# One TensorE-filled kernel, linear attention and a mixture of experts, with its steps in another listed order

## The chip, the cores and the metric

The program runs on one core of a Trainium2 chip. A core has five instruction streams that matter here: TensorE (PE, matmuls into PSUM), VectorE (DVE), ScalarE (ACT), GpSimd (POOL) and SyncE (SP, which only issues transfers). Each works through its own list in order and waits on semaphores for the others. The metric is the device time of one execution in microseconds (us); the time of the kernel before is the median of three runs.

## The reference

For 8 batches of 8 heads, 576 positions and 64 values a head, a linear attention is computed with an exponential feature map of 128 features and its negative. Its output, as 512 values a position, goes through four attention experts with a causal softmax, of which two are chosen and weighted per position. Cut to what is computed:

```
def phi(x):
    proj = einsum('bhsd,df->bhsf', x, w_phi)
    proj = proj - max(abs(proj), axis=-1)
    return concatenate([exp(proj), exp(-proj)])
q_p, k_p = phi(q), phi(k)
kv, z = einsum('bhsf,bhsd->bhfd', k_p, v), sum(k_p, axis=2)
x = (q_p @ kv) / (q_p @ z + 1e-6)            # to [8, 576, 512]
w = softmax over the 2 largest of x @ w_gate
for e in range(4):
    q, k, v = x @ wq[e], x @ wk[e], x @ wv[e]
    a = softmax(causal(q @ k.T / 8))
    out += (w of e) * (a @ v @ wo[e])
```

## The kernel before

Two heads make a pair; there are 32 pairs, four a batch. Every piece of work is a Python generator that yields a `Step` for each instruction or group of instructions that it wants to issue, with the engine it needs, and where it takes a PSUM bank, the tag of the bank. `Plan.loop` (L214) goes through the string `ORDER`: each character names the generator that issues its next step. Where a step may run on ScalarE or VectorE, the string `SIDES` says on which. So the order on each engine is written out by hand, character by character, and `in_order` (L237) ties every engine to it. There are eight PSUM banks of 512 columns, `PSUM_TILES = (("c", 8, 512),)`, and every step of TensorE takes its output bank from them; the bank is free again when the step that empties it has been issued.

The steps on TensorE and their tile shapes, rows by columns of the array, as the traces name them:

- `keep_warm` (L456, matmuls at L294): 21 small matmuls of the tile `warm`, in seven steps of three, into a bank that nobody reads. Shape 128*128.
- `stream_k` and `stream_tails` (L501): projections of a pair's keys (`k_in`, 16 matmuls into two banks) and of the last 64 keys of two pairs (`kt_in`, four matmuls). `stream_q` (L501): projections of queries (`q_in`, four matmuls of 256 and four of 320 columns into four banks). All 64*128.
- `tail_products` (L607, L615): 64*32. `stream_kv` (L642 with `v_in`, L654): keys times values and key sums, 128*32, then transposes at L665, 128*128.
- `stream_n` (L740 denominators, L751 numerators), `sums` (L1038), `attend` (L1067), `gates` (L961): 128*32.
- `proj_t` (`x` with `qk`), `proj_v` (`x` with `vg`) and `out_unit` (`yh`, `yl` with `wo`), all at L294: 128*128.
- `scores` (L871): 64*128, the last 64 keys in 64*64.

A matmul of two `F32` operands stands in the trace as two, one of `F32R` operands (L294, L871) as one. The banks are emptied by VectorE (maximum L566, subtraction L569, copies L315, products and remainders) and ScalarE (copies L303, exponentials L305). Loads go through SP's queue (L327) in the listed order; the first two pairs' queries go through ScalarE's queue. Single buffers, `v_in` among them, are loaded again when their last reader on TensorE is through.

The planner in the file keeps a model of engine times, and `change_cost` in it adds a cost when the shape on TensorE changes. With the order fixed by `ORDER`, that model decides only which free bank a step gets: the one that has been free longest by its times.

Of the kernel before, what the change touches and what calls it, by code (L numbers as in the profile page):

```python
# [17 lines left out]
DM, E = 512, 4  # L18
# [23 lines left out]
LAST = 7  # L42
# [3 lines left out]
WARM = 0   # L46
# [17 lines left out]
def change_cost(a, b):  # L64
# [12 lines left out]
    r'CG8D?5=B<GH6C4:99B2ECMEBEJA8J9886=GJD?>778CMI<HJKI>I<I@<BG39E9C18IHE<A@=8=?E?9G8857?7?EHAJJF083882HGF8ICDHC8DD'
    r'998:C6:GJHI>?I<:JG<1J:7IGH7J:KJGD:?<<BB:BE>@C>;GIIF>L;8>GJGIIJ;8<:=8:HJGHGGJ:IF::LGGK?I=N8=5:=>@K802GQJMM>F:I<'
    r':<0CEEBK=CFE::CFDCDDCJBICDCJCE=D9;;IJHJ<ICIKFHDF4883DD<8<G<<=BBBEI=CCDCDGEFEHGE8BB8D6A8>:I<C5:@@JJ@JEECIAD6BFI'
    r':JK:9FLH9MCLCIJGDHAF9BFAHD8IHBCIE880DH=28BHCB9;ADA@@CA@C@AEL@HB=ECD9;JJBBJD<BGFC;38772J7GF88GG?K=FD<CF895?==A3'  # L80
    r'=8EB888E67FE18D@KHJ@<0E@BCB28=E9988BBDIJID8DGB8848AF<B6<6EE57:7::G=HICLHE3DJDI:::;<BJGC>HD9GHG>B>GADEAF>EEE=8D'
    r'880@C?=B:98:DAF6DIEH8G8GBD9<:::GHHG7BB?NICL5H7B6N=EE;BGC@FI;G=E9?BDJEEBA:<::MGKKDBCG:GC=CD@BIGLMGKFBJH<G:=1348'
    r'8>?EI8IHCA=B;C<<<B>B28>:8:>>>JD>DL8DCBFKJE8::C=<FKEA5G8@:<=HFJHH9<>99AM=6HD?EK==K3@88028K7CJCLFNMKD>?<F?8G887?'
    r'26I88I<AGCC?KJBG<?G=99?8F>H?>F88883AH?E9=I5=F170GIJ@EIKG<=A<DE=HE<7LDB9=<M808<;;C<C6FDCDA99<GGDJ8G@KK7DL85N2GB'
    r'38JGNMGNMHFE?GAG6F><<7:::48E:FF8F8CDFB=E:E:FIJKJ>8FCCCI89B9JIBHI>8:FDDC@D88A::EA3D7F:LFHK8:<II7PHFG?A?@KL@H=5B'
    r'KNN8:6::MPOAMAOGE;E:80:F28E241AKLIJIIFAEEB08=B>ECE8EF:;;89GHH8@@>?5HE6?HI?IHCFBE?B<<<<<GE6BDB>AC?E=CBCB?>:9;@9'
# [179 lines left out]
def tile_linear_attn_moe(ctx, tc, qt, kt, v, wts, out):  # L266
# [925 lines left out]
```

## Time and profile before

| | us |
|---|---|
| median of three runs | 585.22 |
| lowest and highest of them | 584.14, 585.57 |
| profiled execution: span from its first to its last instruction | 582.0 |
| TensorE busy | 568.9 |
| VectorE busy | 533.0 |
| ScalarE busy | 454.3 |
| GpSimd busy | 290.3 |

The profile shows one execution. Its span is what the page counts from the first to the last instruction; the run's time holds some more on both sides, 3.2 us if this execution took what the median did. Busy time is the union of an engine's instructions. In the timeline a piece is a series of like instructions; its start is measured, while the end of a matmul is modelled and contains the drain, so the time that a piece takes from the stream is read from its start to the start of the next piece.

### The profile page before, as it was taken

The page shows a single profiled execution, that of the slowest core. Times are in us where ns is not written, and L with a number is a line of the kernel's source. Part 1 is how long each engine was busy: PE and PEld are TensorE (multiplying, and loading weights), DVE is VectorE, ACT ScalarE, POOL GpSimd, SP SyncE. Part 2 cuts the span into 40 slices and gives each one's busy share as a digit, 9 for nine tenths or more (in the row PEclk, how much of TensorE's full clock was granted, in tenths as well). Part 3 has the DMA queues.
Part 4 walks back from the last instruction along what each step waited for, and adds up shares of the span by engine and source line. Part 5 has one row for each costly group of instructions (what it writes and reads, how often), then busy time and mean ns, then how long its engine had stood idle before and what let it go on. Part 6 is the DMA issues. An engine that isn't in the chain of part 4 may idle for free.

```text
span 582.0 us, 19187 instructions
## 1 busy us (share of the span) xinstructions
PE 568.9 (98%) x7655; PEld 439.9 (76%) x7655; DVE 533.0 (92%) x1150; ACT 454.3 (78%) x1109; POOL 290.3 (50%) x223
## 2 busy tenths in 40 slices
PE   7998999999999999999999999999999999999997
PEld 5664797678785779667876878867888677878886
DVE  7999899999999998999898989989999998898894
ACT  4999888878897969868878877979778678677562
POOL 3737472666336474465554466446635367331430
PEclk9999999999999999999999999999999999999999
DMA  6579656653445753593664663565646432311012
GB/s 164 151 180 212 119 119 141 148 116 95 95 122 136 180 121 55 139 229 76 153 139 102 156 133 107 100 156 134 131 125 148 116 87 46 89 57 43 1 56 110
DMA packets 55049, 69.74 MB, mean 120 GB/s; under 512 B 29232, under 2 KB 32688, under 8 KB 54960
## 3 DMA queue, kind: packets, MB, share of 16 engines
q1 hardware_dynamic: 48368, 49.58, 29.3%
q0 software_dynamic: 6272, 18.35, 19.9%
q8 instruction: 60, 0.98, 0.7%
q10 hardware_dynamic: 320, 0.59, 0.4%
q14 instruction: 29, 0.24, 0.1%
HBM read 35.59 MB, written 14.55 MB: 86 GB/s over the span
## 4 chain that ended last, share of the span: by engine, by line
PE 86%; DVE 6%; DMA 4%; ACT 2%; issue 1%; SPq 0%; ACTq 0%; DVEq 0%
PE ps_c L294 31%; PE ps_c L501 10%; PE ps_c L751 10%; PE ps_c L642 10%; PE ps_c L1067 7%; PE ps_c L871 7%; PE ps_c L740 5%; DMA v_in<-in_v_dram 2%; PE ps_c L654 2%; PE ps_c L607 2%; DVE s L1000 1%; DMA q_in<-in_qt_dram 1%; PE ps_c L1038 1%; DVE u L715 1%; DVE max L1012 1%
## 5 line engine op out<-in xcount | busy, mean ns | idle before, releaser
L713 POOL PARTITION_ALL_REDUCE mx<-u x64 | 145.1, 2289 | 68.2 <-DVE s L1000 17.5
L294 PE MATMUL ps_c<-x,qk 128*128 128x256 f32 (+1 forms) x768 | 108.0, 298 | 0.6 <-DVE yl L298 0.6
L294 PEld LDWEIGHTS ps_c<-x,qk 128*128 128x128 f32 x768 | 102.7, 189 | 4.4 <-issue 0.9
L996 POOL PARTITION_ALL_REDUCE max<-top x16 | 57.7, 3605 | 39.3 <-DVE top L992 18.1
L979 POOL TENSOR_SCALAR_AFFINE_SELECT s<-s 128x256 f32<-128x256 f32 (+1 forms) x80 | 46.4, 626 | 57.3 <-ACT s L303 45.3
L305 ACT ACTIVATE ek<-ek 128x1024 f32<-128x1024 f32 x64 | 67.9, 1061 | 8.0 <-DVE ek L569 7.3
L303 ACT COPY s<-ps_c 64x64 f32<-64x64 f32 (+4 forms) x141 | 52.9, 434 | 17.7 <-PE ps_c L871 17.4
L1000 DVE TENSOR_TENSOR s<-s,max 128x1152 f32<-128x1152 f32 (+4 forms) x80 | 65.5, 853 | 0.6 <-POOL max L996 0.6
L642 PE MATMUL ps_c<-ek,v_in 128*32 128x256 f32 x1024 | 61.7, 381 | 2.2 <-DMA v_in<-in_v_dram 2.2
L305 ACT ACTIVATE s<-s 128x384 f32<-128x384 f32 (+4 forms) x80 | 57.7, 742 | 7.4 <-DVE s L1000 7.1
L294 PE MATMUL ps_c<-yh,wo 128*128 128x256 f32 (+1 forms) x256 | 52.9, 300 | 0.0
L331 POOL DMA_DIRECT2D zs<-ekt x28 | 23.7, 845 | 58.3 <-DVE zs L582 22.4
L642 PEld LDWEIGHTS ps_c<-ek,v_in 128*32 128x32 f32 x1024 | 31.5, 110 | 25.4 <-DMA v_in<-in_v_dram 2.9
L303 ACT COPY u<-ps_c 128x256 f32<-128x256 f32 (+1 forms) x107 | 40.5, 401 | 11.4 <-PE ps_c L501 10.9
L715 DVE TENSOR_TENSOR u<-u,mx 128x576 f32<-128x576 f32 x64 | 48.9, 779 | 0.4 <-POOL mx L713 0.4
L294 PE MATMUL ps_c<-vg,x 128*128 128x260 f32 x384 | 49.0, 285 | 0.2 <-ACT s L303 0.2
L331 POOL DMA_DIRECT2D zs<-ek x28 | 25.4, 906 | 46.1 <-ACT ek L305 29.6
L294 PEld LDWEIGHTS ps_c<-vg,x 128*128 128x128 f32 x384 | 47.1, 188 | 1.2 <-issue 0.5
L1067 PE MATMUL ps_c<-s,vs 128*32 128x320 f32 (+4 forms) x896 | 46.8, 357 | 0.2 <-DVE ek L569 0.2
L501 PE MATMUL ps_c<-q_in,wf 64*128 64x256 f32 (+1 forms) x256 | 42.8, 430 | 3.6 <-DMA q_in<-in_qt_dram 3.2
L566 DVE TENSOR_REDUCE pmax<-ps_c 128x4 f32<-128x512 f32 x64 | 42.4, 681 | 3.8 <-PE ps_c L501 3.3
L305 ACT ACTIVATE mx<-u 128x576 f32<-128x576 f32 x64 | 43.3, 687 | 2.3 <-DVE u L715 2.0
(132 smaller groups left out, 1350.3 us busy)
## 6 DMA issues: line engine op xcount, KB each, us to landing
zs<-ek POOLq DMA_DIRECT2D x28, 512.0 KB, 5.3
out_dram<-ot SPq DMA_DIRECT2D x32, 288.0 KB, 3.0
q_in<-in_qt_dram SPq DMA_DIRECT2D x60, 144.0 KB, 3.6
k_in<-in_kt_dram SPq DMA_DIRECT2D x64, 128.0 KB, 3.4
v_in<-in_v_dram SPq DMA_DIRECT2D x32, 256.0 KB, 3.3
kvd<-kvt SPq DMA_DIRECT2D x104, 48.0 KB, 2.4
kv<-kvd SPq DMA_DIRECT2D x26, 192.0 KB, 2.5
zs<-ekt POOLq DMA_DIRECT2D x28, 128.0 KB, 3.3
```

The source lines that it names most:

```text
L294: nc.tensor.matmul(o, a, b, start=start, stop=stop, skip_group_check=True)
L303: nc.scalar.copy(o, i)
L305: nc.scalar.activation(o, i, func, **kw)
L331: nc.gpsimd.dma_start(o, i, accum_op=ALU.add)
L501: nc.tensor.matmul(o, a, b, start=True, stop=True, skip_group_check=True)
L642: nc.tensor.matmul(o[g, 0:2], v_in[:, 4 * h + t, k:64:2], ek[:, t, :, h, :].rearrange("p c (w f) -> p c w f", w=4), start=False, stop=t == ...
L713: nc.gpsimd.partition_all_reduce(M, U, 128, bass_isa.ReduceOp.absmax)
L715: dve(S, [uk], [mk], port=True).tensor_tensor(out=U, in0=U, in1=M, op=ALU.subtract)
L751: nc.tensor.matmul(ps[g:g + 32, 0:n], kvi[:, 2 * k + (h ^ p % 2), 32 * c:32 * c + 32], P_[h][c][:, s0:s1], start=c == 0, stop=c == 1, skip ...
L996: nc.gpsimd.partition_all_reduce(big.rearrange("p e s -> p (e s)"), top.rearrange("p e s -> p (e s)"), 128, bass_isa.ReduceOp.max)
L1000: dve(2 * (S - 128 * j), [('d', x, j)], [('max', z)], 1.11, True).tensor_tensor(out=block(s_, j, None, rows(j)), in0=block(s_, j, None, ro ...
L1067: nc.tensor.matmul(ps[r:r + 32, q0 - s0:s1 - s0], vs[:, j, 128 * g + 64 * e + k:128 * g + 64 * e + 64:2], ss[x][:, e, o + q0:o + s1], star ...
```

## The change

`ORDER` and `SIDES` are replaced by other strings: the same generators issue the same steps, on the same tiles, with the same transfers, in another order. Of the steps with a choice, two more copies run on VectorE and two fewer on ScalarE. `keep_warm` no longer looks at whether the first part of the first output is done but issues seven steps in any case, as many as it did before; in the new string they all come at the start. Two conditions are written in another way and hold for the same steps: one binds `p` at its definition, the other tests `t < 1` first.

```diff
-WARM = 0 
+WARMS = 7
...
 ORDER = (
-    r'1110049B32894DDBBDCB726C8D99E1B8DF7GD4FEHDH000C=EDBF5CBBB9DC1934DEFE==E98H2=HIHHCED168E<=A541F<77DBIFJCEAE6AHH'
...
+    r'1111111110388C127FFAE3EBA6CDC8C77ED8BAE0FBCC51C<6388CAJAAIADACC4<CAB388H<HI<<EDCBBDGBBAA162G7=J4F3I1KIBI9I5IGH'
...
     def keep_warm():
 
         pk, ps = yield Step('PE', 'c')
-        while ('x', WARM, PARTS[1][0]) not in done:
+        for _ in range(WARMS):
             yield Step('PE')
             for _ in range(3):
                 mm(ps[:, 0:128], warm, warm, True, True, 128, pk, [])
...
-            plan.spawn(fractions('d', p, ps, pk, 1e-6, xf, ['xf'], (lambda: all(('xd', p - 1, s0) in done for s0, s1 in PARTS)) if p else None, ('rb', p)))
+            plan.spawn(fractions('d', p, ps, pk, 1e-6, xf, ['xf'], (lambda p=p: all(('xd', p - 1, s0) in done for s0, s1 in PARTS)) if p else None, ('rb', p)))
...
-                pk, ps = yield Step('PE', 'c', lambda: ('w', 3) in done and ('y', 2 * b, s0) in done and (('av', 2 * b + 1) in done or t < 1 if b >= LAST else ('y', 2 * b + 1, s0) in done))
+                pk, ps = yield Step('PE', 'c', lambda: ('w', 3) in done and ('y', 2 * b, s0) in done and (t < 1 or ('av', 2 * b + 1) in done if b >= LAST else ('y', 2 * b + 1, s0) in done))
```

Two places of TensorE's list, before and after. In the rows `ps_c_64` and the like are PSUM banks, the number behind other names is the buffer, and the last item is the shape of the output.

TensorE, the end of what stands between the fifth and the sixth group of line 642 (the group that reads `v_in`); before:

```order
L501 MATMUL ps_c_67<-wf,k_in_102 128x128
L501 MATMUL ps_c_70<-wf,k_in_102 128x128
L501 MATMUL ps_c_65<-q_in_105,wf 128x256
L501 MATMUL ps_c_63<-q_in_105,wf 128x256
L665 MATMUL ps_c_64<-ident,kvt 128x128 x3
L642 MATMUL ps_c_68<-ek_108,v_in 32x2x4x32 x16
```

Now the same end of the stretch; the rows are the first that follow the key projection:

```order
L501 MATMUL ps_c_64<-wf,k_in_102 128x128
L501 MATMUL ps_c_69<-wf,k_in_102 128x128
L665 MATMUL ps_c_68<-ident,kvt 128x128 x3
L294 MATMUL ps_c_70<-x_143,qk 128x256 x3
L294 MATMUL ps_c_70<-x_144,qk 128x256 x3
L294 MATMUL ps_c_70<-x_145,qk 128x256 x3
L294 MATMUL ps_c_70<-x_146,qk 128x256 x3
L294 MATMUL ps_c_64<-x_143,qk 128x320 x3
L294 MATMUL ps_c_64<-x_144,qk 128x320 x3
L294 MATMUL ps_c_64<-x_145,qk 128x320 x3
L294 MATMUL ps_c_64<-x_146,qk 128x320 x3
L740 MATMUL ps_c_68<-mx_133,kv_118 32x288
```

Before, the group of line 642 came three rows behind the key projection. Now eight rows of line 294 and eight of line 740, of which the first is shown, stand in between.

TensorE, the fifth projection of key tails (`kt_in`); before, between the tail products of line 607 and the numerators of line 751:

```order
L607 MATMUL ps_c_66<-ekt_112,vt_in 32x2x4x32
L607 MATMUL ps_c_64<-ekt_112,vt_in 32x2x4x32
L501 MATMUL ps_c_70<-wf,kt_in 128x128
L501 MATMUL ps_c_68<-wf,kt_in 128x128
L751 MATMUL ps_c_63<-mx_133,kv_118 32x256 x2
L751 MATMUL ps_c_63<-mx_134,kv_118 32x256 x2
```

Now, behind a key projection and ahead of the scores of line 871:

```order
L501 MATMUL ps_c_65<-wf,k_in_102 128x128
L501 MATMUL ps_c_70<-wf,k_in_102 128x128
L501 MATMUL ps_c_67<-wf,kt_in 128x128
L501 MATMUL ps_c_63<-wf,kt_in 128x128
L871 MATMUL ps_c_66<-qh_158,kkh_160 128x448
L871 MATMUL ps_c_69<-qh_158,kkh_160 128x448
```

Before, its two rows had another tile shape in front of them and another behind; now all three pieces have 64 rows and 128 columns.

## Rows read from the trace of the kernel before

**Rows 1.** The page, sections 1 and 2: busy us and share; granted TensorE clock by slice

```profile
PE 568.9 (98%) x7655; PEld 439.9 (76%) x7655; DVE 533.0 (92%) x1150; ACT 454.3 (78%) x1109; POOL 290.3 (50%) x223
...
PEclk9999999999999999999999999999999999999999
```

**Rows 2.** Waits of TensorE: who waited for what: us in total, times, longest

```profile
PE ps_c L501 <- DMA q_in<-in_qt_dram: 3.2, 2, 3.0
PE ps_c L642 <- DMA v_in<-in_v_dram: 2.2, 2, 1.7
PE ps_c L294 <- DVE col L338: 1.1, 1, 1.1
```

**Rows 3.** Stretch: its us, busy us (x count) of PE, PEld, DVE, ACT, POOL; clock; DMA

```profile
20.00:100.00 80.00, 78.04 (x1109) 57.00 (x1108) 75.04 (x147) 70.67 (x154) 43.38 (x30) 1.00 0.68 154
100.00:200.00 100.00, 99.51 (x1394) 74.38 (x1390) 96.76 (x208) 84.10 (x213) 52.72 (x41) 1.00 0.55 127
```

**Rows 4.** TensorE's timeline, 45 to 57 us: start us, us, engine line op names

```profile
45.41 0.67 PE L740 MATMUL ps_c<-mx,kv 128*32 128x288 f32 x8
45.89 0.67 PE L740 MATMUL ps_c<-u,kv 128*32 128x288 f32 x8
46.49 1.24 PE L501 MATMUL ps_c<-q_in,wf 64*128 64x256 f32 x8
47.66 0.66 PE L607 MATMUL ps_c<-ekt,vt_in 64*32 64x256 f32 x16
48.26 1.94 PE L642 MATMUL ps_c<-ek,v_in 128*32 128x256 f32 x32
...
56.03 1.29 PE L642 MATMUL ps_c<-ek,v_in 128*32 128x256 f32 x20 [1.67 <-DMA v_in<-in_v_dram]
```

**Rows 5.** TensorE's timeline, 161 to 166 us

```profile
161.92 0.56 PE L294 MATMUL ps_c<-yh,wo 128*128 128x320 f32 x2
162.32 0.31 PE L294 MATMUL ps_c<-yl,wo 128*128 128x320 f32 x1
162.47 0.46 PE L294 MATMUL ps_c<-yh,wo 128*128 128x320 f32 x2
162.76 0.31 PE L294 MATMUL ps_c<-yl,wo 128*128 128x320 f32 x1
...
164.35 0.31 PE L294 MATMUL ps_c<-yl,wo 128*128 128x320 f32 x1
164.59 0.41 PE L871 MATMUL ps_c<-qh,kkh 64*128 64x320 f32 x2
```

**Rows 6.** TensorE's timeline, 165 to 167 us

```profile
165.33 0.37 PE L871 MATMUL ps_c<-qh,kkl 64*128 64x448 f32 x2
165.54 0.37 PE L871 MATMUL ps_c<-ql,kkh 64*128 64x448 f32 x2
165.74 0.19 PE L871 MATMUL ps_c<-qh,kkh 64*64 64x64 f32 x2
```

**Rows 7.** The chain of waits, 50 to 57 us: start us, us, what

```profile
50.25 5.73 DMA v_in<-in_v_dram
```

**Rows 8.** TensorE's timeline, the first 15 us

```profile
1.06 1.14 PE L294 MATMUL ps_c<-warm 128*128 128x128 bf16 x9 [1.06 <-DVE col L338]
5.22 1.22 PE L501 MATMUL ps_c<-q_in,wf 64*128 64x256 f32 x4 [3.03 <-DMA q_in<-in_qt_dram]
...
8.85 1.18 PE L501 MATMUL ps_c<-q_in,wf 64*128 64x256 f32 x8
9.82 0.38 PE L501 MATMUL ps_c<-wf,k_in 64*128 64x128 f32 x2
...
11.51 0.68 PE L294 MATMUL ps_c<-warm 128*128 128x128 bf16 x9
12.12 0.66 PE L607 MATMUL ps_c<-ekt,vt_in 64*32 64x256 f32 x16
```

**Rows 9.** The page, section 5: VectorE pass per bank of key projections

```profile
L566 DVE TENSOR_REDUCE pmax<-ps_c 128x4 f32<-128x512 f32 x64 | 42.4, 681 | 3.8 <-PE ps_c L501 3.3
```

More of the change, by code (lines that the diff above doesn't have):

```diff
@@ L77 @@
[L77 to L86, printed above, removed]
@@ new lines @@
+    r'EF=G<4BBBB7<7=88HAF6DGHIEF<<<=JFKDBJ9KIA<1692AI97II<EEI<9GH<IH===IKF4MG9H1BGG9GGC<6F9H7E;;F7EAH3388DDH;G@EADJF'
+    r'@0EFFB;;G;IBBABA77F134::EIA209F8E8B3AKDE;;:?KGECCHHDAGBD:4967@J0HGG5KKKKDFF@E?B?=::==GDGC=B;@8GCDD8CEAD9DD::8C'
+    r'B97G5DFE9<<<21F3G0HHDE?66?@ABG>DDDFEA@@CC9C999<877H@AIBGGCFC:9G88;HH;IH@=5I6MJDCD;;JLLE>GKJHFBAADFEE;:E;;EEECF'
+    r'BAAC6@GGG;C=GBEC>B??>=?8886=308;8882;@0?482=1A=3A50;DDB===A@B@A@::::99889EDDA<<<>@>GDAC?A8888DDCCA84388B:AA:F>'
+    r'DF7KE5BAI7MLIB6MIMHEJ998888BL<<2@>8>>9IF@<8HAA<GFFC<G999E>EG@C@B@85E=8?EFF377DDIBJK<CCD@EB6AFB<A=<B9F=@@B<9>><'
@@ new lines @@
+    r'<;::;6?BB?:EE:<::C>ECE00882>ECCABAA777:ACCD7CEGEEECDF@A:G@FGF<?F<<F<@<E18888838888889I8:JJF::I:LIE>?DH6HH14BDD'
+    r'AB=HG;HII5D:KGG::L:CC6GG?K?CJFE22CEEFCFIFGC@ECC;;IHDF8;88<<:<<<G=?GI>FFFF6<AFEBDBCBBBAAC<JJMBJKKCF<ECDEEEEF0B:'
+    r'E:I<:I5FH:3M9HEGFECHHHE@@EDFC9D9GEDEDCDHDBGH@CF@@@CHCGEB8888@8883JHE@8D?8G?D=<@==09C;988AC8BD8CBB9CB7DD7D28D<7'
+    r'EE<??50AB761FEFKE<8@A<KKEEGEKGCA9;9M@FIKC88H9FIJ66E5;F>F:7J87LEG23EK4FAF<FF@88>BB8<>:D:::<::J>888KEB@EIE@IDG3A'
+    r'A8BEFE:G:6=JEAFG=G>8C@FB?FF9FEE9B::BEFHF5E:7DDKKB288808:8:F6=>GEDD?EE=EHIGBEEB84319ECAECCBFAA;?;8@7CHF5KEEC=F:'
@@ new lines @@
+    r'NAH=C@B@:=KDGGF<<JA<8<H;@:E<E6EEK?>>@E?D>DD@>F>>>LBBA>>@99NO9P<B>GIHBHCHH:JJ:J:M@M:CMIBFAA<7PP888KIAAHFHJ@D082'
+    r'888853GGFE678HL>FL9I9IG880<>9H=I8?BIJ8IDE@888I123H=@HBB@C@=A4=E=8?E998C88EEFCFECCD6<E=><DD80<D8C::<B:=5=E==<<E'
+    r'=>D7ML77MO67PBBC::::DIOOFDBB28F@@LHBAAJ<>9@=DI@;BI==;;<?E?GEG0HF9HG=?FE988>38C88>8=C9CC=:EED?@B==BDA5=?7H7;IED'
+    r';BAG=C>HHIC08888@D@F:ED8HFHCC;6IHHH5::023=EBCH?EM<LLMM:6BNIHFHEB=G:JG:GDGGAA<:DF:GGBAHFEAE?6?=C<<<9998??<48888'
+    r'21>>>>@@>?D?AA::>ABEACDD>HA>DC<>772HAGFE?=C8838::>:CH=GGGIH?8@C@?5699KNJND@FD?A9888888380J4IGJIBFIDJIF8=JJGG?G'
@@ new lines @@
+    r'99888HG77217HHJI50AIIK7ELOO9QEE?6?GBOL@IIIB=DDBBB??KKK9L9D6=<A<IIJ=:::HDLL<DII?:::K<HF>>@:<B?FFFC>>>>=GGF>EFEA'
+    r'<M<L888888883C828BB7ML567QQ2<IK;L9@R>LMRQOQEDCKHBHJ;LH:::;LBQK6@N@NBHDG=::::MO:N:LDJKJJ>BBBB@CHHHAHH6HCJL>KIDF'
+    r'EB48AHFFGBH8GFAAA:88;;:I:MIKC5:DKG:;DDNCJJJ3M<MMIH>PNE?F=CG<K@HEE<<<999IG???EEJ1A<BAHAFFCHA0088888883E?C?E<8C8'
+    r'57LLEC>7JJC6>N==M<<F?2<AJJFADCCCI999=888K888LAMMAA=GIBEIJBBJ9E?E9HFFGAH988<B<<HA<FBGHF6@ICI<778888827LGL04LI3M'
+    r'MBCE<CK<5<<O7<>6KNBM9AG:9DE?GNAO:::::POHALHEEENIEMKEMGJG=G8GFIDI8:G8=@=C21F=88I8F83GDBH=;;:HHIHIHH;7<L872MNKH:'
@@ L101 @@
+    r'86677777348444473:854022:20000?2?0059;2<:438965551100036566650335694798406330607130545030544343114644355440004'
+    r'338?779<3330@:::<<<595:555111:0855552766666133166123144133333541<331<51581114521231331325434443102021113321121'
+    r'0004>>==12:7>=010;22180811126403020010'
 )
 SIDES = (
[L104 to L105 removed]
@@ L109 @@
+    r'01000000000000101000000000000001000110010000000000000000001000000100100000000000100000010000000010000000100100'
+    r'00000000000001100000000000000000001001000000000000101000000001010000000000001000100000000000001101000110110000'
+    r'01001000000001000000000100001000000001000100100000000000000000000000000001110001'
 )
```

30 lines of the change are left out of this document (7 added, 23 removed).

## The prediction

> **What bounds the kernel now.** I read the page first, then the list of who waited for whom, then busy time by stretch, then the timeline of TensorE piece by piece. TensorE (PE) is busy for 568.9 of 582.0 us [rows 1]. That alone doesn't prove that it sets the end, so the list of its waits comes next [rows 2]: 3.2 us in two waits for the first queries, 2.2 us in two waits for `v_in`, 1.1 us before the very first instruction, and five further lines, each shorter than that. By stretch, from 20 to 100 us TensorE is idle for 80 - 78.04 = 1.96 us, and from 100 to 200 us for 0.49 us [rows 3]. VectorE (DVE) is full too, 96.76 of 100 us in the second of these stretches, but TensorE waits for it there for less than half a microsecond. So TensorE's own stream is the bound, and a cheaper stream shortens the kernel as long as the other engines keep up.
>
> What a reader must see next is that the stream holds time in which no columns pass. Two pieces of line 740 stand behind each other, of the same eight matmuls [rows 4]: the first starts at 45.41 and the next piece at 45.89, 0.48 us later; the second starts at 45.89, but the projection of line 501 that follows, of another tile shape, starts at 46.49, 0.60 us later. The 0.12 us between them is the price of leaving the shape 128*32.
>
> **Price of a change of shape.** A price has two halves, leaving one shape and entering the other. All are differences from start to start, since the printed length of a piece holds the drain.
> - Leaving 128*32: 0.60 - 0.48 = 0.12 us [rows 4].
> - Entering and leaving 64*128: the query projection takes 47.66 - 46.49 = 1.17 us between two other shapes [rows 4]; the same eight matmuls take 9.82 - 8.85 = 0.97 us where the shape is 64*128 before and behind [rows 8]. Both halves: 0.20 us.
> - Entering 128*128: the first two `yh,wo` matmuls behind line 871 take 162.32 - 161.92 = 0.40 us, the next two of that kind 162.76 - 162.47 = 0.29 us [rows 5]: 0.11 us.
> - Leaving 128*128: the last `yl,wo` takes 164.59 - 164.35 = 0.24 us, an earlier one 162.47 - 162.32 = 0.15 us [rows 5]: 0.09 us.
> - Inside the scores the shape goes from 64*128 to 64*64; the last pair ahead of it takes 165.74 - 165.54 = 0.20 us and the pair before that 165.54 - 165.33 = 0.21 us [rows 6]. That costs nothing, so I count 64*64 as 64*128.
> - Entering 128*32 or 64*32: I put it at nothing.
>
> **The change, part by part.** Along TensorE's listing I counted how often each shape is entered. 128*32: 60 times before, 54 after. 128*128: 44 and 36. 64*128 (with 64*64): 61 and 47. 64*32: 16 and 16. Changes in all: 181 and 153, that is 28 fewer. The sum: 6 x 0.12 = 0.72; 8 x (0.11 + 0.09) = 1.60; 14 x 0.20 = 2.80; together 5.1 us. One visit to 128*128, worth 0.2 us, is that of the warm-up matmuls at 11.51 us and belongs to the start, below. So 4.9 us lie on the path that sets the end. Reading the starts to 0.01 us leaves 0.02 to 0.03 us on each price, so 28 changes may be worth from 4.2 to 5.7 us.
>
> [...]
>
> **The warm-up matmuls.** Of 21, nine now stand at 1.06 us, nine at 11.51 us and three later; afterwards all 21 stand first. At the pace of the first nine (1.14 us) [rows 8] they take 2.7 us and are through by 3.8 us, ahead of the first query data, for which TensorE waits until 5.22 us anyway. The wait for the DMA hides them. What they leave behind is 12.12 - 11.51 = 0.61 us at the second place and some 0.2 us for the other three. If that cover were gone they would cost 1.5 us at the start. Line 607 and those behind it may then wait for their own operands (the exponentials of the first keys come through VectorE and ScalarE), so the gain is between 0 and 0.8 us; I take the middle, 0.4.
>
> [...]
>
> **The load of `v_in`.** There is one such buffer, and its next load waits for the last matmul of line 642. Before, that group ends at 48.26 + 1.94 = 50.20 us and the next starts at 56.03 us after waiting for 1.67 us [rows 4]; the chain of waits shows the transfer, 5.73 us from 50.25 us [rows 7]. The stretch thus had 5.83 - 1.67 = 4.16 us of other work, and needed 5.83. Afterwards the listing has 24 matmuls of line 294 there as well (12 of 320 columns at 0.15 us, a start-to-start time in [rows 5], and 12 of 256 at 0.12 in proportion: 3.2 us) and eight rows of line 740 (2 x 0.48 us). That is 8.3 us, and the wait goes: -1.7 us. The tightest pair in the new listing, between the groups that read the 17th and the 18th load, has some 5.4 us of work between them; a transfer as long as the one above would bring back 0.4 us. SP's queue holds the same transfers as before, each behind others, so a load can start late; that is in the next term.
>
> **New waits.** Every hand-over stands in a new place. Between 0 and 4.9 us of what is won can come back as waits for VectorE, ScalarE or a load. I take 1.8 us: the value nearest to the 1.96 us of the stretch from 20 to 100 us [rows 3], and far from the high end, since 0.49 us in 100 us is all that TensorE lost where VectorE was fullest.
>
> **How that adds up.** -4.9 - 0.4 - 1.7 + 1.8 = -5.2 us on the profiled span of 582.0 us, so 576.8 us. The median of the runs is 585.22 us, 3.2 us above that span for what lies around it; I leave that as it is: 580.0 us.
>
> **Rivals.**
> 1. Banks run out. Fewer changes of shape mean longer runs of one kind of step. A run in 64*128 fills PSUM banks quickly and VectorE empties them: a bank of key projections needs a maximum of 0.68 us [rows 9] and a subtraction that I put at the same. There are eight banks. In the listing 8 of 61 such runs fill eight banks or more before, 13 of 47 after. If each of the 13 waited for one bank, that is 1.36 us each, 17.7 us in all, and the kernel would stand at 585.2 - 7.0 + 17.7 = 595.9 us. It turns slower by over 0.3%, about what a measurement of this kernel can tell from no change, when 7.0 + 1.8 = 8.8 us are lost, at some 6 of the 13 runs. For it: VectorE at 96.76 of 100 us [rows 3]. Against it: eight such runs were there before, and no wait of TensorE for VectorE in the body comes near 1.36 us [rows 2, 3]. I give it 0.11 to be slower.
> 2. The change does less than it says: the shape prices go, but TensorE meets VectorE and ScalarE earlier and waits as long in the end. If all 4.9 us come back, 0.4 + 1.7 stay, and 583.1 us result; with the lost `v_in` wait replaced too, 584.8 us. VectorE is idle for 582.0 - 533.0 = 49 us over the span [rows 1], which speaks against a full return. 0.13 for ending within 0.3%.
> [...]
>
> **How the numbers follow.** The forecast, 577 to 583.4 us, gets 0.70; rival 3 adds 0.06. So faster 0.76, within 0.3% 0.13, slower 0.11. The low end of the range: shape price 5.7, warm-up 0.8, `v_in` 2.2 and no new waits make -8.7 us, 576.5 us. The high end takes in rival 2 and the mild part of rival 1: 585.0 us. Beyond it lie some 0.13, below the low end 0.06.
>
> **What would show it.** In the profile after: TensorE's mid-kernel pieces at the same start-to-start times as here, with 0.12 and 0.20 us steps at the changes that are left; all warm-up matmuls ahead of 4 us and a first projection near 5.2 us; no wait of 1 us or more for `v_in` between 45 and 60 us; TensorE idle between 20 and 560 us by no more than some 4 us. The prediction is wrong if that idle time is over 8 us, above all in lines 501 and 871 behind VectorE or ScalarE, or if the busy time of TensorE falls by much less than 4 us.

## The result and the profile after

The changed kernel takes 590.75 us (median; 590.67 to 591.63) beside 584.68 us of the kernel before on the same chip: a ratio of 1.0119, with a 95% interval of 1.0096 to 1.0142. It is slower; the forecast was 580.0 us with 585.0 us as the high end. The profiled execution has a span of 589.8 us, 7.8 us more than before; it is the longest of the four, and the spans of the others are 588.9 and 589.0 us. The medians lie 6.1 us apart. In nearly all executions on record the run's time is 1.7 to 1.9 us above the span, so the execution profiled before probably took some 583.8 us, less than its median, and the 3.2 us that the prediction's last sum carries are not a fixed surcharge. The page of the changed kernel, sections 1, 2 and 4 (busy us by engine; granted TensorE clock by slice; the chain of waits by engine):

```profile
PE 571.6 (97%) x7655; PEld 445.3 (75%) x7655; DVE 545.4 (92%) x1152; ACT 453.6 (77%) x1107; POOL 287.1 (49%) x223
...
PEclk9998999999999999999999999999999999999999
...
PE 67%; DVE 17%; issue 4%; DMA 4%; SPq 2%; ACT 2%; POOL 2%; ACTq 0%; DVEq 0%; POOLq 0%
```

The same line of section 4 for the kernel before:

```profile
PE 86%; DVE 6%; DMA 4%; ACT 2%; issue 1%; SPq 0%; ACTq 0%; DVEq 0%
```

Two things stand out against [rows 1]. VectorE is busy for 12.4 us longer (545.4 instead of 533.0), with two copies more in 1152 operations. And its share of the chain that sets the end has gone from 6 to 17%. TensorE's waits after the change, the longest lines (who waited for what: us in total, times, longest):

```profile
PE ps_c L501 <- DMA q_in<-in_qt_dram: 2.4, 1, 2.4
PE ps_c L654 <- DMA zs<-ekt: 1.9, 1, 1.9
PE ps_c L961 <- DVE col L952: 1.6, 1, 1.6
PE ps_c L294 <- DVE ekt L557: 1.4, 1, 1.4
...
PE ps_c L871 <- ACT s L303: 0.7, 1, 0.7
PE ps_c L1067 <- DVE kkl L298: 0.7, 1, 0.7
...
PE ps_c L642 <- DMA v_in<-in_v_dram: 0.3, 1, 0.3
```

The 2.2 us for `v_in` [rows 2] are down to 0.3, as forecast. But TensorE, which reads neither `ekt` nor `kkl` in the lines that wait there, now waits for VectorE to be through with them: it wants the bank of PSUM that VectorE still reads. I sorted every wait of over 0.1 us behind the first 20 us by whether the operation waited for reads the bank that TensorE is to write ("for a bank") or makes an operand. Waits for a bank: 5 before with 1.4 us, 13 after with 5.9 us, of which 11 with 4.6 us are behind VectorE and two behind ScalarE. Waits for operands: 3.4 us before, 4.1 us after. By stretch, first the changed kernel, then the sum line for the kernel before (us of the stretch, busy us of PE, PEld, DVE, ACT, POOL, clock, DMA):

```profile
20.00:100.00 80.00, 77.91 (x1083) 58.18 (x1087) 74.37 (x144) 72.78 (x157) 43.80 (x30) 0.98 0.64 153
100.00:200.00 100.00, 97.26 (x1382) 73.17 (x1375) 96.02 (x205) 80.53 (x208) 53.90 (x41) 1.00 0.54 126
200.00:560.00 360.00, 356.39 (x4710) 280.34 (x4709) 339.63 (x711) 275.28 (x685) 175.51 (x140) 1.00 0.46 110
sum 540.00, PE 531.56 PEld 411.70 DVE 510.03 ACT 428.59 POOL 273.22; mean PE 177.19 PEld 137.23 DVE 170.01 ACT 142.86 POOL 91.07
```

```profile
sum 540.00, PE 536.00 PEld 412.88 DVE 503.04 ACT 432.66 POOL 280.67; mean PE 178.67 PEld 137.63 DVE 167.68 ACT 144.22 POOL 93.56
```

Between 20 and 560 us TensorE is idle for 540 - 531.56 = 8.4 us, against 4.0 us before. "Over 8 us" was the mark that the prediction set for being wrong. It came, but hardly in lines 501 and 871, which the prediction named: they hold 1.5 of the 8.4 us. The other mark came too: TensorE's busy time did not fall by 4 us but rose by 2.7.

**Where the time came from.** I priced each run of equal matmuls in both traces by what the same run takes, start to start, where nothing is waited for in the trace of before, with the prices of a change of shape. At those prices TensorE's stream needs 564.1 us before and 558.5 us after: 5.6 us less, of which 4.9 us for the changes of shape; the rest is about what the twelve warm-up matmuls took that no longer stand behind the first useful one (nine took 0.61 us [rows 8]). This is an estimate from those rows. What stands beyond the prices grew from 8.3 to 20.7 us, by 12.4 us. The first useful matmul starts 0.6 us later and the end lies 0.5 us further behind the last matmul. -5.6 + 12.4 + 0.6 + 0.5 = +7.9, the 7.8 us of the spans. (These 12.4 us and the 12.4 us of VectorE's busy time are two different sums.) By slice of 20 us the growth is 1.1 us in the first, 1.9 from 40 to 60, 3.1 from 140 to 160, 1.1 from 200 to 220, 2.0 from 320 to 340, the rest in small pieces.

**What is late.** The clearest of these places, on all engines' common timeline of the changed kernel (start us, us, engine line op):

```profile
329.25 2.37 DVE L715 TENSOR_TENSOR u<-u,mx 128x576 f32<-128x576 f32 x1
329.42 2.44 POOL L713 PARTITION_ALL_REDUCE mx<-u  x1
...
331.54 0.68 DVE L569 TENSOR_TENSOR ek<-ps_c,pmax 128x512 f32<-128x512 f32 x1
...
332.28 0.51 PE L294 MATMUL ps_c<-yh,wo 128*128 128x256 f32 x2 [0.30 <-DVE ek L569]
```

A subtraction of line 715 (`u` minus its maximum, both in SBUF) begins, GpSimd begins the maximum of another head 0.17 us later, and the subtraction takes 2.37 us. Undisturbed it takes 0.75 us: its median away from GpSimd's maxima, 745 ns (the expectations below say 0.72). It ends 0.24 us before the maximum does. Line 569, which empties a bank, starts only then, and TensorE waits for that bank. The kernel's own text knows of such meetings, and the prediction made no use of it: `in_order` (it stands at L245) lets each maximum wait for the VectorE operation with two inputs in SBUF that is listed last ahead of it, and for an operation listed behind the maximum the planner's model adds waiting time (L153). So the listing has a say in which operations meet a maximum. The worst cluster, VectorE's timeline and then TensorE's:

```profile
140.22 1.87 DVE L715 TENSOR_TENSOR u<-u,mx 128x576 f32<-128x576 f32 x1
...
144.87 1.86 DVE L715 TENSOR_TENSOR u<-u,mx 128x576 f32<-128x576 f32 x1 [0.47 <-POOL mx L713]
...
148.60 1.56 DVE L715 TENSOR_TENSOR u<-u,mx 128x576 f32<-128x576 f32 x1
```

```profile
147.56 2.03 PE L294 MATMUL ps_c<-x,qk 128*128 128x320 f32 x12 [1.39 <-DVE ekt L557]
...
150.82 0.86 PE L1067 MATMUL ps_c<-s,vs 128*32 128x256 f32 x16 [0.60 <-DVE ek L569]
152.35 1.01 PE L1067 MATMUL ps_c<-s,vs 128*32 128x320 f32 x12 [0.67 <-DVE kkl L298]
```

Line 715 as a group, before and after (busy us, mean ns):

```profile
L715 DVE TENSOR_TENSOR u<-u,mx 128x576 f32<-128x576 f32 x64 | 48.9, 779 | 0.4 <-POOL mx L713 0.4
```

```profile
L715 DVE TENSOR_TENSOR u<-u,mx 128x576 f32<-128x576 f32 x64 | 59.6, 941 | 0.5 <-POOL mx L713 0.5
```

Below, the **stretch** of a trace is the time that VectorE's operations take beyond the median of their line and size (that median taken away from GpSimd's maxima), summed over those that are over by 0.06 us. It is 12.2 us before and 22.2 us after, and 12.8 us of the latter are line 715. So 10.0 of the 12.4 us by which VectorE is busy longer are stretch. Not every stretched operation lies beside a maximum: in the kernel before, a subtraction at 142.93 us takes 1.74 us while GpSimd runs line 979.

### The profile page after: what moved, and what is told of

Read it like the earlier page. It is cut to its first block, busy times and chain, and to the rows that moved or that the text cites. A ratio compares the mean times of both kernels' runs of the same rounds, so it can differ in the third digit from the quotient of the medians.

```text
span 589.8 us, 19173 instructions
## 1 busy us (share of the span) xinstructions
PE 571.6 (97%) x7655; PEld 445.3 (75%) x7655; DVE 545.4 (92%) x1152; ACT 453.6 (77%) x1107; POOL 287.1 (49%) x223
## 4 chain that ended last, share of the span: by engine, by line
PE 67%; DVE 17%; issue 4%; DMA 4%; SPq 2%; ACT 2%; POOL 2%; ACTq 0%; DVEq 0%; POOLq 0%
PE ps_c L294 25%; PE ps_c L501 9%; PE ps_c L751 8%; PE ps_c L642 7%; PE ps_c L1067 6%; PE ps_c L871 5%; PE ps_c L740 4%; SPq L327 2%; DVE u L715 2%; DVE pmax L566 2%; DVE top L992 2%; PE ps_c L654 1%; DVE ek L569 1%; DMA out_dram<-ot 1%; PE ps_c L607 1%
## 5 line engine op out<-in xcount | busy, mean ns | idle before, releaser
L979 POOL TENSOR_SCALAR_AFFINE_SELECT s<-s 128x256 f32<-128x256 f32 (+1 forms) x80 | 42.8, 589 | 66.0 <-ACT s L303 63.9
L1000 DVE TENSOR_TENSOR s<-s,max 128x1152 f32<-128x1152 f32 (+4 forms) x80 | 63.8, 835 | 1.8 <-POOL max L996 1.8
L305 ACT ACTIVATE s<-s 128x1152 f32<-128x1152 f32 (+4 forms) x80 | 56.9, 743 | 6.2 <-DVE s L1000 5.9
L715 DVE TENSOR_TENSOR u<-u,mx 128x576 f32<-128x576 f32 x64 | 59.6, 941 | 0.5 <-POOL mx L713 0.5
L303 ACT COPY s<-ps_c 128x256 f32<-128x256 f32 (+4 forms) x144 | 53.0, 432 | 6.0 <-PE ps_c L871 5.6
L303 ACT COPY u<-ps_c 128x320 f32<-128x320 f32 (+1 forms) x110 | 40.3, 405 | 15.3 <-PE ps_c L501 14.9
L1067 PEld LDWEIGHTS ps_c<-s,vs 128*32 128x32 f32 x896 | 29.4, 110 | 21.5 <-DVE kkl L298 1.1
```

The source lines that it names most:

```text
L303: nc.scalar.copy(o, i)
L305: nc.scalar.activation(o, i, func, **kw)
L715: dve(S, [uk], [mk], port=True).tensor_tensor(out=U, in0=U, in1=M, op=ALU.subtract)
L1000: dve(2 * (S - 128 * j), [('d', x, j)], [('max', z)], 1.11, True).tensor_tensor(out=block(s_, j, None, rows(j)), in0=block(s_, j, None, ro ...
L1067: nc.tensor.matmul(ps[r:r + 32, q0 - s0:s1 - s0], vs[:, j, 128 * g + 64 * e + k:128 * g + 64 * e + 64:2], ss[x][:, e, o + q0:o + s1], star ...
```

## The experiments

Theory A: these collisions with GpSimd's maxima make VectorE late where the banks are full, and this is what the new order costs. Rival B, the first one of the prediction: longer runs of one shape fill the banks at any speed of VectorE. Beside them stood smaller questions: the start, the wait at 52 us, and whether a collision or merely VectorE's total time matters.

**1 and 2. Short maxima, in both kernels.** The edit, the same in each:

```diff
-        nc.gpsimd.partition_all_reduce(M, U, 128, bass_isa.ReduceOp.absmax)
+        nc.gpsimd.partition_all_reduce(M[:, 0:64], U[:, 0:64], 128, bass_isa.ReduceOp.absmax)
+        nc.gpsimd.memset(M[:, 64:S], 0.0)
```

> The changed kernel, with GpSimd's maximum of line 713 taken over 64 of the 576 columns (the other 512 maxima are left out and filled with zero), so that GpSimd is occupied for much less than the 2.1 us of each of the 64 maxima. Theory A (collisions): in the changed kernel VectorE's operations from SBUF to SBUF that meet the start of such a maximum are stretched, line 715 from 0.72 us to as much as 2.3 us; VectorE's busy time is 545.4 us against 533.0 us before, and banks of PSUM are emptied late. Then the mean of line 715 falls from 941 ns to some 760 ns, VectorE's busy time to some 533 us, TensorE's waits for a bank at 144 to 152, 324 to 334 and 433 us (5.9 us in all, 1.6 us before) go, and the span of 589.8 us falls to between 582 and 586 us. Theory B (runs): long runs of one tile shape fill the eight banks whatever GpSimd does; then these waits stay above 4 us and the span stays above 588 us.

> The kernel before, with the same cut: the maximum of line 713 over 64 of 576 columns, the other 512 left out and filled with zero. Both theories expect little, since TensorE waits only 1.6 us for banks there: a span of 580.5 to 582 us. Theory A expects the mean of line 715 to fall only from 779 to some 750 ns, and the difference between the two kernels, 7.8 us with full maxima, to shrink to between 1 and 5 us when both have short ones (what is left is the start and the wait at 52 us); theory B expects it to stay between 6 and 8 us.

Measured: the changed kernel with short maxima 583.2 us, a ratio to the kernel before of 0.9972 (0.9951 to 0.9993); the kernel before with short maxima 584.14 us, 0.9990 (0.9972 to 1.0008). Spans 579.8 and 582.1 us: the first is 2.2 us below the range of theory A, and the difference of the two is -2.3 us where theory A had 1 to 5 and theory B 6 to 8. The page of the first (section 1) and five lines of its waits:

```profile
PE 565.6 (98%) x7655; PEld 442.7 (76%) x7655; DVE 530.8 (92%) x1152; ACT 452.3 (78%) x1107; POOL 212.7 (37%) x287
```

```profile
PE ps_c L654 <- DMA zs<-ekt: 2.0, 2, 1.8
PE ps_c L962 <- DVE col L953: 1.6, 1, 1.6
PE ps_c L872 <- DVE kkl L298: 1.3, 1, 1.3
...
PE ps_c L872 <- ACT s L303: 0.7, 1, 0.7
PE ps_c L962 <- ACT ot L303: 0.5, 1, 0.5
```

The page of the second:

```profile
PE 570.3 (98%) x7655; PEld 441.6 (76%) x7655; DVE 526.3 (90%) x1150; ACT 454.2 (78%) x1109; POOL 219.0 (38%) x287
```

The cut takes 10.0 us off the changed kernel's span (7.5 us off its median) and nothing off the other's. The stretch falls to 5.2 and 4.2 us, and of the waits for a bank that VectorE empties none is left in the changed kernel: the 48 matmuls `x,qk` that stood still for 1.39 us behind the 36th (at 147.56 us) go through without a gap, with the same run of scores and key projections ahead of them. That speaks for A and against B. One wait for VectorE is new, 1.3 us at 90.9 us for an operand of line 298; 4 us ahead of it a subtraction takes 2.66 us beside a maximum of line 996, which the edit did not cut. The two pages also bear on the shape term: TensorE is busy for 570.3 and 565.6 us, 4.7 us apart. That is no measurement of this term alone, for TensorE still waits (it is idle for 3.1 and 4.9 us between 20 and 560 us), and short stops under the modelled end of a matmul count as busy. The edit shortens GpSimd's work by some 75 us besides, so experiment 5 keeps all of it.

**3. The warm-up matmuls alone**, in the kernel before:

```diff
 listing of TensorE
+warm-up matmuls 10 to 21
 q projection, pair 0
...
-warm-up matmuls 10 to 18
...
-warm-up matmuls 19 to 21
```

(the banks are given by a table that keeps each one where it was; so in every kernel below whose listing is changed)

> The kernel before with one part of the change alone: all 21 warm-up matmuls in front of the first useful matmul, everything else in its old place and in the same banks. The prediction's step: they are hidden by the wait for q_in, the first projection still starts at 5.22 us, and the span falls by 0 to 0.8 us from 582.0 us. Rival (the later rise of the pace in the changed kernel, 11.33 us instead of 8.19 us, comes from where the warm-ups stand): the pace rises after 9.5 us, and the span grows by 0.5 to 2 us.

Measured: 585.04 us, ratio 1.0005 (0.9988 to 1.0021). No difference that this can tell: the interval reaches from 0.7 us faster to 1.2 us slower. The first projection started at 4.95 us, so the wait does hide the warm-ups. The pace, which shows in the time that TensorE's matmuls take from start to start, rose at 10.5 us: fifteen key matmuls take 1.70 us from 7.46 us on, sixteen take 1.15 us from 10.80 us on. This fits the rival's words on the pace; of its price, 0.5 to 2 us, the lower half is not excluded. And the pace is no property of the order: in the kernel with short maxima, whose start is that of the kernel before, it rose at 10.7 us (the 128 query matmuls of 256 columns take 417 ns in the mean, in the first profile 409), where it had risen at 8.2 us in the first profile.

**4. The old start under the new order.** The listing up to 16 us is that of before; the rest follows in the new order.

> The changed kernel, in which all that the kernel before lists up to 16 us of its trace comes first and in that kernel's order on every engine (the warm-ups in their old places too); the rest follows in the changed order. Theory S (the start costs on its own): first projection at 5.2 us instead of 5.83 us, pace up at 8.2 us instead of 11.33 us, and 1.5 to 2 us less than the span of 589.8 us. Rival (absorbed): the 2 us are swallowed by the wait for the sum of the keys at 52 to 55 us, which hangs on VectorE and on GpSimd's queue and not on TensorE, and the span falls by less than 0.5 us.

Measured: 592.34 us, ratio 1.0145 (1.0118 to 1.0173), span 590.3 us. The first projection starts at 4.90 us, 0.9 us ahead of the changed kernel, but that is gone by 40 us: the same matmuls of line 642 start at 39.80 us here and at 39.72 us in the changed kernel. The longest wait of this kernel:

```profile
PE ps_c L664 <- DMA zs<-ekt: 2.7, 2, 2.5
```

(line 664 is line 654 here.) It had been 1.9 us: TensorE comes there 0.1 us later than in the changed kernel, and the transfer lands 0.7 us later (55.24 us instead of 54.54). The start is not what the change costs: the span did not fall, it is 0.5 us longer. So theory S falls. The rival, which had a fall of less than 0.5 us, is right in that and wrong in where the time goes, since it is gone ahead of this wait.

**5. Later maxima, all work kept.** Ten maxima of the changed kernel are listed behind the VectorE operation that they met, so that by `in_order` each waits for it. One of the ten:

```diff
 listing of VectorE and GpSimd
-GpSimd   maximum, pair 23, head 0     (line 713)
 VectorE  subtraction, pair 21, head 0 (line 715)
+GpSimd   maximum, pair 23, head 0     (line 713)
```

> The changed kernel with its full maxima, in which ten of GpSimd's maxima of line 713 are listed directly behind the VectorE operation that they stretched in the profile (10 of the 15 places where an operation was stretched by over 0.25 us; these ten hold 12.5 of the 22.2 us), so that each waits for that operation. TensorE's, VectorE's, ScalarE's and the DMA queues' own orders and all banks stay. Theory A (collisions): the stretch in VectorE falls from 22.2 to some 10 us, the waits for a bank at 147 to 152 us and 324 to 334 us go, and the span falls from 589.8 us to between 581 and 586 us. Rival D (it was the shorter occupation of GpSimd, hence earlier maxima, that helped when the maxima were cut, not the collisions): maxima that come even later help nothing, and the span stays at 588 us or more.

Measured: 587.46 us, ratio 1.0045 (1.0026 to 1.0064), span 585.5 us, stretch 14.4 us. Line 715, here line 725, is back:

```profile
L725 DVE TENSOR_TENSOR u<-u,mx 128x576 f32<-128x576 f32 x64 | 50.7, 801 | 0.3 <-POOL mx L723 0.3
```

Waits for banks are 3.9 us instead of 5.9: those at 210 and from 324 to 334 us are gone, and the 1.39 us at 147.56 too, but two of those behind it stay (0.7 and 0.8 us) and a wait at 429 us grew to 1.1 us, as the maxima moved there met others. The stretch fell by 7.8 us and not by 12, and the span by 4.3 us, into the range of theory A. Maxima that come later made the kernel faster by 3.3 us, so rival D falls: it was not their earlier end that helped in experiment 1.

**6. More work for VectorE in the old order.**

```diff
         dve(S, [uk], [mk], port=True).tensor_tensor(out=U, in0=U, in1=M, op=ALU.subtract)
+        if (p, h) in MORE:
+            for _ in range(2):
+                nc.vector.tensor_tensor(out=U, in0=U, in1=U, op=ALU.max)
```

> The kernel before, with two more passes of VectorE over u (the maximum of u with itself, which changes nothing) behind line 715 at those ten places (pairs of heads 0, 5, 11, 12, 19, 21, 27, 29) whose subtraction was stretched in the changed kernel: 20 operations of some 0.72 us, 13 to 14 us more work in VectorE, the 12.4 us that its busy time grew by. Theory A in its plain form (VectorE's time is what TensorE loses, whatever the order): the span grows by 3 to 6 us from 582.0 us, with new waits for banks. Theory C (the old order has room for it, and only the longer runs of one shape make the new one wait): the span grows by less than 1.5 us.

Measured: 596.42 us (two executions, 595.0 and 597.83), ratio 1.0192 (1.0141 to 1.0243). VectorE's busy time is 15.5 us up and the kernel 10.9 us slower, well over what theory A had put (3 to 6 us). Its page and three of its waits that are not among those of the kernel before (its lines stand 2 to 5 further down):

```profile
PE 577.2 (97%) x7655; PEld 445.0 (75%) x7655; DVE 548.5 (92%) x1170; ACT 454.5 (76%) x1109; POOL 289.3 (49%) x223
```

```profile
PE ps_c L503 <- DVE ek L571: 1.8, 2, 1.5
PE ps_c L1043 <- DVE max L1017: 1.4, 2, 0.9
PE ps_c L1043 <- POOL mx L715: 1.1, 1, 1.1
```

The old order has no room for it either: theory C falls. An order with short runs suffers from a late VectorE too. (The profiled execution holds two stretches of 3.4 us at a granted clock of 0.50, at 21.1 and 62.1 us; the other execution, with a mean clock of 0.999, is the one of 595.0 us.)

**7 and 8. Less work for VectorE, collisions kept**, in both kernels:

```diff
-tensor_reduce(out=m[:, us], in_=src, axis=AX.X, op=ALU.max, apply_absolute_value=True)
+tensor_reduce(out=m[:, us], in_=src[:, :, 0:64], axis=AX.X, op=ALU.max, apply_absolute_value=True)
```

> The kernel before, with VectorE's maximum of line 566 taken over 64 of the 128 features of each row (the others are left out), 64 operations shorter by some 0.27 us: 17 us less work in VectorE, while GpSimd's maxima and what they stretch stay. Theory A: TensorE has 1.6 us of waits for banks to give back, so the span falls by 0.5 to 2.5 us from 582.0 us.

> The changed kernel with the same cut of line 566 (64 of 128 features, the others left out). Theory A (VectorE's time has become the bound): VectorE's busy time falls from 545 to some 528 us, most of the 5.9 us of waits for banks go, and the span falls from 589.8 us to between 581 and 585 us, within 2 us of before_light. Theory B (runs of one shape fill the banks at any speed of VectorE): the waits for banks stay above 4 us, and the span stays above 587 us.

Measured: before 583.63 us, ratio 0.9971 (0.9951 to 0.9990), as expected. After 588.76 us, ratio 1.0069 (1.0043 to 1.0094), span 586.5 us: a miss, 1.5 us above the expected range. VectorE's busy time fell by 14.7 us, to 530.7 us, the same as in experiment 1, yet the time fell by 2.0 us and not by 7.5. Theory B missed it as well: it had a span above 587 us and waits for banks above 4 us. Page of this kernel, and three of its waits:

```profile
PE 569.3 (97%) x7655; PEld 443.6 (76%) x7655; DVE 530.7 (90%) x1152; ACT 452.8 (77%) x1107; POOL 283.8 (48%) x223
```

```profile
PE ps_c L654 <- DMA zs<-ekt: 2.3, 1, 2.3
...
PE ps_c L294 <- DVE ekt L557: 0.5, 1, 0.5
PE ps_c L1067 <- DVE kkl L298: 0.4, 1, 0.4
```

Its stretch is 22.3 us, as large as in the changed kernel, and 3.4 us of waits for banks stay, at the same places (145.6 to 149.8, 321 and 329 us). So the sum of VectorE's work is not the cause in itself. I read it thus: what counts is 1 to 1.6 us at once, in front of an operation that empties a bank while TensorE has no other bank to go on with; a quarter of a microsecond saved at each of 64 other places makes up for that only in part. No run varies the length of a single delay.

**9. The subtraction on GpSimd**, in both kernels, directly behind its maximum:

```diff
-        dve(S, [uk], [mk], port=True).tensor_tensor(out=U, in0=U, in1=M, op=ALU.subtract)
+        plan.run('POOL', 1000, [uk], [mk])
+        nc.gpsimd.tensor_tensor(out=U, in0=U, in1=M, op=ALU.subtract)
```

> The changed kernel with the subtraction of line 715 done by GpSimd itself, directly behind its maximum; all other orders and all banks stay. Theory A: VectorE loses 60 us of its 545 us and most of the collisions with it, TensorE's waits for banks go, and the span falls to between 578 and 584 us. Rival E: GpSimd's own subtractions are long (over 1.5 us) and hold VectorE up in the same way, or the features u come late; then the span stays at 588 us or grows.

> The kernel before with the same move of line 715 to GpSimd. Theory A: few waits for banks are there to be saved, so the span falls by 0 to 2 us from 582.0 us, and the changed kernel ends 1 to 5 us ahead of it. Rival E: slower than before.

Measured: 1383.19 and 1361.3 us (the latter one execution), spans 1382.9 and 1359.5 us. Theory A missed it; rival E has the sign, but not the reason or the size. GpSimd's timeline in the changed kernel with this edit (start us, us, engine line op, idle time before):

```profile
100.73 1.39 POOL L726 TENSOR_TENSOR u<-u,mx 128x576 f32<-128x576 f32 x1 [6.67 <-issue]
107.99 2.15 POOL L723 PARTITION_ALL_REDUCE mx<-u  x1 [5.87 <-issue]
117.51 1.39 POOL L726 TENSOR_TENSOR u<-u,mx 128x576 f32<-128x576 f32 x1 [7.36 <-issue]
```

Each of these subtractions takes 1.39 us, but 5.9 to 7.4 us pass at the three changes between it and the maximum, in either direction, in which GpSimd waits for nothing that the profile shows. Ahead of all 64 subtractions GpSimd is idle for 454.8 us, 7.1 us each, and for 419.4 us of them the page names no releaser ("issue"). In the kernel before a maximum, line 979 and a transfer can follow each other on GpSimd without such a gap: a maximum from 102.98 us for 2.14 us, line 979 from 105.01 us; a transfer into `zs` from 117.54 us for 0.90 us, a maximum from 118.43 us. What fills the gaps was not shown. This says nothing on whether collisions are the cause; it closes the way to relieve VectorE here.

**10. The wait at 52 us: is the transfer too large?** Experiment 1's kernel with one edit more:

```diff
-add_to(o[r], ekts[m % 2][r].rearrange("p c h f -> p (c h f)"), k, tk, 700, 0.5)
+add_to(o[r, 0:64], ekts[m % 2][r].rearrange("p c h f -> p (c h f)")[:, 0:64], k, tk, 700, 0.5)
```

> The changed kernel with the maxima of line 713 cut to 64 columns (the rest zero, as in after_short), and besides the sum of the tail keys into zs cut to 64 of 512 columns (the other tail keys are left out of the denominators), so that this transfer on GpSimd's queue has an eighth of its bytes. If the 1.8 us that TensorE still waits at 51.6 us hang on that transfer's size, the wait goes and the span falls from 579.8 to 578 us or a little less. Rival G (the transfer is late because others are in flight on the same queues): the wait shrinks by less than 0.6 us.

Measured: 582.33 us, ratio 0.9951 (0.9925 to 0.9976), span 580.5 us. TensorE's timeline:

```profile
54.51 0.42 PE L654 MATMUL ps_c<-zs,ones 128*32 128x128 f32 x8 [1.59 <-DMA zs<-ekt]
```

1.59 us instead of 1.84, and from issue to landing the transfer takes 5.59 us instead of 5.84, while the median of its kind falls from 3.4 to 2.8 us: with an eighth of the bytes it is about as late as before. Rival G's number holds. What else is in flight is in the order of the loads: in the changed kernel three loads of weights are issued at 47.25, 47.88 and 48.48 us, and this transfer, issued at 48.64 us, lands at 54.54 us, where its kind takes 3.3 us in the median before. That these loads delay it was not tried by itself.

**11. Further repair.** Eight of the ten moves of experiment 5, one of them replaced, and four more on VectorE and GpSimd, from the places that were left:

```diff
 listing of VectorE and GpSimd, 46 to 50 us
+VectorE  sum of keys, line 582
+GpSimd   sum of tail keys into zs, line 331
 GpSimd   maximum, pair 5, head 0
...
-VectorE  sum of keys, line 582
-GpSimd   sum of tail keys into zs, line 331
```

> The changed kernel repaired further, from what the last runs showed. Eight maxima of GpSimd are listed later as in after_par_later, the maximum of pair 11, head 0 now behind the sum of keys at 153 us; the last addition of the row maxima at 147 us stands ahead of the subtraction that it was stretched behind; and at 46 to 50 us the addition of line 582 and the sum of tail keys that follows it go ahead of one maximum, so that the transfer that TensorE waits for at 52 us is issued some 1 us earlier. TensorE's own order and all banks stay. Theory A: stretch in VectorE 10 to 12 us (22.2 in the changed kernel, 14.4 in after_par_later), the wait at 52 us falls by 0.5 to 1.5 us, span 582 to 584.5 us against 585.5 us of after_par_later: level with the kernel before. Rival F (each removed collision turns up as another, since every order meets some): stretch stays at 14 us or more and the span at 585 us or more.

Measured: 585.87 us, ratio 1.0011 (0.9986 to 1.0036), span 584.2 us. The wait at 52 us fell from 2.3 to 1.4 us and the span lies in theory A's range. But the transfer was not issued earlier (48.65 us, against 48.64 in the changed kernel), and the stretch stayed at 14.2 us: one removed collision came back as another (1.4 us at 149.5 us), as rival F had it. The time is level with the kernel before by the interval; all ten runs have a mean clock of 0.998 or more, and beside the 16 runs of the kernel before on this chip that do (median 584.2 us) this kernel is 1.7 us slower. No version that does all the work was faster than the kernel before.

## Why the prediction was wrong

**Right: the price of a change of shape.** 28 changes fewer were put at 4.9 us, between 4.2 and 5.7. The steps stand in the changed kernel as before: eight matmuls of line 740 take 0.485 us where the shape stays (median of 43 there, of 46 before) and 0.598 us where it changes (13 and 15). A pair's key projection takes 0.85 us within its shape and 1.09 us between two others in the kernel before, so the 0.20 us for 64*128 are on the low side. With GpSimd's maxima cut the busy times differ by 4.7 us. TensorE's stream did become cheaper by about what was forecast.

**Right in the sum, in part by luck: `v_in`.** The wait of 1.67 us at 56.03 us is gone, and 0.3 us for `v_in` are left, nearly the 0.4 of the tightest pair. But this wait is not in that pair. The 18th load took 3.05 us and nobody waited for it; the wait is ahead of the 27th group, whose load was issued late, at 411.23 us. What was not seen is that a wait as long came up in line 654, until 54.67 us.

**Not decided: the warm-ups.** -0.4 us was forecast, and experiment 3, whose interval is 2 us wide, can't tell that from nothing. In the changed kernel the first useful matmul starts at 5.83 and not at 5.22 us, since its data land later, but experiment 4, which starts at 4.90 us, has lost that lead by 40 us.

**Wrong: "So TensorE's own stream is the bound, and a cheaper stream shortens the kernel as long as the other engines keep up".** This is the step that failed. TensorE is busy for 98% [rows 1], and it waited for VectorE by less than half a microsecond in the stretch where VectorE was fullest [rows 3]; from this I took it that the other engines would keep up. The rows show that VectorE kept up in the old order, not that its operations would take as long and come as early in another. In the new order it was busy for 12.4 us longer, and TensorE's waits for banks grew from 1.4 to 5.9 us. How much VectorE has to do in all does not settle it either way: in experiment 6 15.5 us more cost 10.9 us in the old order, but in experiment 8 14.7 us less, with the collisions left in, gave back 2.0 us. Of the 49 us that I named as VectorE's idle time only 8.2 us (180 - 75.04 - 96.76) lie between 20 and 200 us [rows 3], where 5.0 us of the growth arose in two slices.

**Wrong in size and kind: new waits, +1.8 us.** They were put between 0 and 4.9 us, from how little TensorE waits in the old order. The 1.96 us from which the 1.8 were taken are, in the trace of before, the 1.67 us for `v_in`, which the sum counts by themselves, and 0.29 us behind ScalarE. The bound had no row behind it that says how long VectorE's own operations will take in another order. "Same instructions" was read as "same busy time"; it was 12.4 us more, 10.0 of them because the time of an operation depends on what GpSimd does beside it. The trace of before had this in it: a group of line 715 whose mean is 779 ns where its undisturbed time is 745, and single operations of lines 1000 and 1012 that take 0.9 to 1.9 us more than their like. The waits, the time around each, the half pace of one stretch (below) and the later rise of the pace at the start took back 12.4 us where 1.8 were set down.

In the two traces it is operations that read two tiles in SBUF that suffer: lines 566 and 569, which read a bank, keep their mean (681 and 672 ns before, 676 and 677 ns after), and lines 715, 1000 and 1012 carry 19.4 of the 22.2 us of stretch. The place beside the maximum counts: of 20 operations of lines 582, 715, 774, 992 (`top<-top,s`), 1000 and 1012 that start within 1.3 us behind the start of a maximum of line 713, 13 are stretched by over 0.25 us, but of 48 that start 1.3 to 2.3 us behind it, while most of the maxima still run, only 2. Who starts first does not settle it by the profile, which calls its spans on GpSimd rough: of subtractions that begin 0.1 to 0.4 us ahead of a maximum five of five take 0.75 to 0.76 us in the kernel before, but four of five take 2.10 to 2.37 us in the changed one. What holds these operations up was not shown.

**Rival 1 came nearest.** Banks did run out, at 13 places with 5.9 us, and the kernel came out slower. But its mechanism, long runs that fill eight banks, is not enough by itself: in experiment 1 the same runs go through without a wait for a bank behind VectorE. The price per place of 1.36 us fits only one of the thirteen. (Counted in the traces, 16 runs of 64*128 write eight banks or more before and 25 after, not 8 and 13.) **Rival 2** had the sign nearly right for its own reason ("TensorE meets VectorE earlier"), and stopped at a full return of the gain, where the return was more than twice the gain. **Rival 3**, which has 0.06 among the chances, was an earlier rise of TensorE's pace at the start, put at 1.8 us by an estimate of mine; no run shows that gain. The pace rose later, at 11.3 us instead of 8.2: sixteen key matmuls take 1.15 us from 7.70 us on in the kernel before, and 1.71 us from 8.31 us on in the changed one.

**What stays open.** How much of the time each wait costs beyond itself was not tried by itself: waits between 20 and 560 us grew by 4.4 us of idle time, and the excess over the prices in the same stretch by more. And no run shows the new order with all its work and few collisions at once: experiment 11 has 2 us more of stretch than the kernel before and is level or 1.7 us behind, not 5 us ahead. Part of that is not a matter of collisions with the maxima of line 713. Three waits stand in the changed kernel and in its versions of experiments 1, 5, 8 and 11 alike: 0.4 to 0.5 us behind the copy of `ot`, 0.7 us behind the copy of `s`, and 1.6 us behind `col`, where the kernel before has 0.8. So do 1.4 to 2.3 us for the transfer into `zs`. No experiment took them away, and what the order would gain without them is open.

## What to carry to other kernels

A listing that is moved keeps its instructions but not their durations (line 715: 779 ns in the mean before, 941 after): before a reordering is priced, look in the trace for operations of one line and size that differ in length, and for what ran beside the long ones. An engine that is hardly waited for is not thereby an engine with room (experiment 6: 15.5 us more on VectorE, 10.9 us more in all). Its busy time in all doesn't say it either: in experiments 1 and 8 VectorE is busy for 530.8 and 530.7 us, and the spans are 6.7 us apart. Where two engines pass banks to each other, one delay of a microsecond in front of the operation that frees one seems to cost more than many small ones elsewhere. And a planner's model that stands in the kernel's text can name an effect that the rows show only in single operations.

## What the runs showed of the hardware that I had not expected

- In the changed kernel a subtraction that begins 0.17 us before a maximum on GpSimd, at 329.25 us, takes 2.37 us instead of 0.75 and ends 0.24 us before the maximum does; in experiment 8 one at 325.95 us that begins 0.31 us before takes 2.51 us. The places come back: two kernels of the same order stretch the same operations by the same amounts (1.18, 0.99 and 0.99 us between 131 and 147 us, in the kernel before and in experiment 3).
- In experiment 9 the three changes shown between a maximum over partitions and a subtraction on GpSimd take 5.9 to 7.4 us each; between such a maximum and line 979 the kernel before shows no such gap (102.98 to 105.12 us and from 105.01 us on).
- TensorE's granted clock fell to half in the middle of the changed kernel. By stretch and piece:

```profile
55.70:59.10 3.40, 3.40 (x27) 3.18 (x24) 2.27 (x5) 3.36 (x8) 1.16 (x1) 0.50 0.85 226
```

```profile
55.86 1.93 PE L501 MATMUL ps_c<-wf,k_in 64*128 64x128 f32 x16
```

The granted clock is 0.50 for 3.4 us, right behind the wait of 1.89 us at 52 us; sixteen matmuls take 1.86 us to the next start, where fifteen of the same kind take 1.07 us at 140.21 us. Half of 3.4 us, some 1.7 us, is lost, and it is not tied to the order: it followed a wait of 1.72 us in experiment 3, not one of 2.29 us in experiment 8, and among 69 runs of the kernel before 31 have a mean clock of 0.997 or less, with medians of 585.6 to 585.9 us by chip, where those at 0.999 or more have 583.6 to 584.1 us.
